# Moving the transposes of k, q and y from TensorE to VectorE seven units earlier (y: six), in an mLSTM cell with a multiplicative FFN

One core of a Trainium2 chip. The metric is the device time of one execution in microseconds (us), the median of several; lower is better.

## The reference

An mLSTM cell (4 batches, 8 heads, 768 positions, head size 40) feeds a feed-forward block without a nonlinearity but with a product of two projections. The cell's data are float32. The weights of the block come as 64-bit floats; the kernel reads them as pairs of 32-bit words and computes in float32.

```python
for t in range(S):                                    # the cell, per batch and head
    m_new  = max(f_gate[t] + m, i_gate[t])
    f_stab = exp(f_gate[t] + m - m_new);  i_stab = exp(i_gate[t] - m_new);  m = m_new
    C = f_stab * C + i_stab * outer(v[t], k[t])       # 40 x 40 state
    n = f_stab * n + i_stab * k[t]
    y[t] = sigmoid(o_gate[t]) * (C @ q[t]) / max(abs(n @ q[t]), 1)

x = y as (B*S, H*D) = (3072, 320)
out = (((x @ w1) * (x @ w2)) @ w3) @ w_out            # 320 -> 1024 -> 1024 -> 320
```

## The kernel before

The sequence is cut into 24 units of 128 rows of one batch. The cell is computed by blocks: for every unit TensorE forms scores from k and q, products with v, and state updates. Because w3 and w_out have nothing between them, the kernel first multiplies them (`wp`: one 128 x 320 block per step from turned words of w3), and uses `w3o = w3 @ w_out` for all rows.

k, q and y of every unit are turned (transposed) ahead of TensorE's products with them, and the kernel has two ways of doing it. In the first, TensorE transposes through PSUM (`pt` for k and q, 1.02 us for eight, `px` for y, 0.33 us for three, in step 13) and ScalarE copies the result out (0.59, 0.59 and 0.50 us). In the second, VectorE turns them (1.09 us for k and for q, 0.57 for y); for that k and q are loaded a second time as rows in a special layout, and y makes a trip through DRAM. `N_DVE` and `NY` say from which unit on the second way is used.

The weights come in pieces of words. For each piece ScalarE scales the upper words, and VectorE makes float32 numbers of it in four instructions (a conversion); a piece of w3 is turned by a fifth.

```python
N_DVE = 17                                   # k, q: VectorE from unit 17 on
NY = 15                                      # y: VectorE from unit 15 on
# one home for the rows, in the memory of the gates:
turned_in = [gates[:, i * TB:(i + 1) * TB] for i in range(2)]

def turn(n):                                 # cut
    if n >= N_DVE:
        for src, dst, name in zip(turned_in, (kT_t, qT_t), ("kT", "qT")):
            dst[n] = sb.tile([128, NP, P], FP, name=name, tag=name)
            nc.vector.transpose(out=..., in_=...)
        return
    ...                                      # TensorE: 8 transposes, 2 copies by ScalarE

def convert():                               # one piece of words on VectorE (cut)
    if not scaled:
        scale_next()                         # ScalarE: scaling of the raw words, "raw<-raw"
    dst, raw, ko, half = scaled.pop(0)
    ...
    w3 = wst.tile([128, CW], FP, name="w3", tag="w3")
    to_f32(w3, raw)                          # 4 instructions: ex, ma, ma, w
    ...
    nc.vector.transpose(out=w3T_t[ko]..., in_=w3...)
```

The main loop; a pass of it is a step. The order of statements is the order of the program text. The build then decides in which order each engine's instructions are queued, within what the data demands; `tc.issue_after(x)` is an edge that forbids it to queue an instruction ahead of x on the same engine. VectorE works its queue off in order, as the 4.36 us below show, in which it stands with ready work further back in its queue.

```python
for s in range(len(n_up)):                   # cut
    load_u(s + 3); load(s + 2); load_o(s + 2)
    ...
    if 0 < s < N_DVE: turn(s)                # TensorE's way
    if NY <= s - 2 < NU: send(s - 2)         # y out to DRAM
    if N_DVE <= s + 1 < NU: load_turned(s + 1)   # rows of k and q, 8 transfers
    if NY <= s - 2 < NU: get_back(s - 2)     # y back in turned layout
    ...
    open_ups = [up(*x) for x in now]         # the projections pa, pb
    gated = quarter_work(s, rest)            # rest(): end of pa, pb and VectorE's product ab;
                                             # then the cell, h, den, y on VectorE
    with tc.issue_after(gated.ins):
        if NY <= s - 2 < NU: x_turn(s - 2)   # VectorE turns y
        if N_DVE <= s + 1 < NU: turn(s + 1)  # VectorE turns k and q
    ...
    for _ in range(n_cvt[s]): convert()      # 2 pieces in each of steps 9 to 15, then none
    while todo and fetched < converted + (2 if s < 2 else 3):
        fetch(*todo.pop(0))                  # words of weights, from DRAM
```

## Time and profile before

| | before |
|---|---|
| median time of the first three executions | 474.29 us (473.12 to 476.47) |
| span of the profiled run | 474.2 us |
| TensorE busy | 450.0 us, 95% of the span |
| VectorE busy | 241.0 us, 51% |
| start of wp's first product in step 10 and in step 17 | 120.20 and 237.69 us |

The lines that say most (chain, steps, groups) stand in the prediction. Two more lines of the page will be wanted, TensorE's busy time and the granted clock in tenths of full speed over 40 slices of the span:

```profile
PE 450.0 (95%) x5375; PEld 362.3 (76%) x5375; DVE 241.0 (51%) x501; ACT 142.4 (30%) x390; POOL 84.2 (18%) x156
...
PEclk9995999999999999999999999999999999999999
```

The change acts in the steps 10 to 17, and the **wp interval**, from the start of wp in step 10 to its start in step 17, holds what it does there, 237.69 - 120.20 = 117.49 us.

### The profile page before, as it was taken

How to read it: one execution, taken by the hardware profiler on the slowest of the kernel's cores; microseconds unless marked ns; L12 is line 12 of the kernel's file. 1: busy time of each engine (PE TensorE's matmuls, PEld its weight loads, DVE VectorE, ACT ScalarE, POOL GpSimd, SP SyncE). 2: the span in 40 equal slices, each digit the busy share in tenths (PEclk: the TensorE clock that was granted, in tenths of full speed). 3: DMA queues.
4: the chain of work that ended last, by engine and by line, in shares of the span. 5: the costliest groups of instructions: out<-in, count | busy, mean ns of one | idle time of the engine just before them, and what ended most of it. 6: DMA issues, size and time to landing. Idle time of an engine off the chain costs nothing.

```text
span 474.2 us, 12856 instructions
## 1 busy us (share of the span) xinstructions
PE 450.0 (95%) x5375; PEld 362.3 (76%) x5375; DVE 241.0 (51%) x501; ACT 142.4 (30%) x390; POOL 84.2 (18%) x156
## 2 busy tenths in 40 slices
PE   2867999899999999999999999999999999999997
PEld 2766878788878888788878787787877778768864
DVE  6676698988865766785351523515236043111110
ACT  3643545544243263344331212211101111011111
POOL 5341333521220222213220211100000000000000
PEclk9995999999999999999999999999999999999999
DMA  7999978599987756432452546354240220200001
GB/s 174 181 166 173 214 138 157 118 201 194 185 165 111 167 104 149 85 65 55 82 121 61 122 105 136 58 127 88 61 116 11 53 43 20 62 14 15 1 15 41
DMA packets 135770, 49.28 MB, mean 104 GB/s; under 512 B 116320, under 2 KB 126752, under 8 KB 135712
## 3 DMA queue, kind: packets, MB, share of 16 engines
q1 hardware_dynamic: 132112, 44.42, 47.8%
q10 hardware_dynamic: 3600, 4.03, 2.5%
q8 instruction: 42, 0.69, 0.6%
q14 instruction: 16, 0.13, 0.1%
HBM read 42.63 MB, written 5.80 MB: 102 GB/s over the span
## 4 chain that ended last, share of the span: by engine, by line
PE 82%; DVE 7%; issue 7%; POOL 2%; ACT 1%; DMA 0%; SPq 0%; DVEq 0%; POOLq 0%
PE pa L90 23%; PE po L90 22%; PE pb L90 16%; PE cell L90 9%; PE wp L90 7%; PE pt L93 2%; DVE h L371 1%; PE ub L90 1%; ACT pw L277 1%; PE px L93 1%; DVE o_in L381 1%; POOL state L306 1%; DVE y L383 1%; DVE h L367 1%; DVE den L378 1%
## 5 line engine op out<-in xcount | busy, mean ns | idle before, releaser
L567 DVE TENSOR_TENSOR ab<-pb,a_sb 128x512 f32<-128x512 f32 x48 | 33.1, 691 | 159.8 <-ACT a_sb L566 159.6
L90 PE MATMUL po<-w3o,ab 128*128 128x320 f32 x384 | 106.2, 435 | 0.0
L90 PEld LDWEIGHTS po<-w3o,ab 128*128 128x128 f32 x384 | 72.1, 190 | 30.1 <-issue 0.4
L90 PE MATMUL pa<-xT,w 128*128 128x256 f32 x384 | 91.1, 380 | 0.6 <-ACT xT L421 0.6
L90 PE MATMUL pb<-xT,w 128*128 128x256 f32 x384 | 90.8, 379 | 0.0
L90 PEld LDWEIGHTS pa<-xT,w 128*128 128x128 f32 x384 | 72.3, 190 | 13.3 <-ACT xT L421 1.0
L90 PEld LDWEIGHTS pb<-xT,w 128*128 128x128 f32 x384 | 72.9, 190 | 10.2 <-ACT kT L296 0.3
L566 ACT ACTIVATE a_sb<-pa 128x512 f32<-128x512 f32 x48 | 28.6, 595 | 149.4 <-PE pb L90 149.4
L90 PE MATMUL pa<-xT,wr 64*64 64x256 f32 x384 | 47.0, 383 | 0.0
L90 PE MATMUL pb<-xT,wr 64*64 64x256 f32 x384 | 47.0, 383 | 0.0
L277 ACT ACTIVATE pw<-pw,aT 128x64 f32<-128x64 f32 x160 | 40.8, 338 | 18.1 <-DMA pw<-U_d 18.1
L279 POOL TENSOR_SCALAR_AFFINE_SELECT pw<-pw 64x512 f32<-64x512 f32 x48 | 35.8, 745 | 52.5 <-ACT pw L277 51.0
L306 POOL TENSOR_TENSOR state<-state,decay 128x164 f32<-128x164 f32 x40 | 19.5, 491 | 139.7 <-issue 53.6
L90 PEld LDWEIGHTS pa<-xT,wr 64*64 64x64 f32 x384 | 25.8, 132 | 16.8 <-issue 7.8
L90 PE MATMUL wp<-wo,w3T 128*128 128x320 f32 x128 | 35.8, 432 | 0.0
L574 ACT COPY o_sb<-po 128x320 f32<-128x320 f32 x24 | 10.2, 423 | 76.6 <-PE po L90 76.4
L90 PEld LDWEIGHTS cell<-vbuf,pw 64*64 64x64 f32 x768 | 27.7, 142 | 6.2 <-issue 2.0
L90 PEld LDWEIGHTS wp<-wo,w3T 128*128 128x128 f32 x128 | 23.7, 190 | 8.9
L90 PE MATMUL cell<-vbuf,pw 64*64 64x41 f32 x768 | 27.6, 232 | 2.4 <-issue 1.4
L347 DVE TENSOR_TENSOR pw<-cell,pw 128x512 f32<-128x512 f32 x24 | 16.5, 686 | 21.7 <-PE cell L90 21.7
L90 PEld LDWEIGHTS pb<-xT,wr 64*64 64x64 f32 x384 | 25.8, 132 | 0.0
L371 DVE TENSOR_TENSOR h<-cell,h 64x328 f32<-64x328 f32 x48 | 23.8, 497 | 1.1
(88 smaller groups left out, 463.4 us busy)
## 6 DMA issues: line engine op xcount, KB each, us to landing
raw<-in_moe_w_dram SPq DMA_DIRECT2D x64, 128.0 KB, 3.2
pw<-U_d SPq DMA_DIRECT2D x40, 128.0 KB, 4.1
kbuf<-in_k_dram SPq DMA_DIRECT2D x24, 160.0 KB, 4.6
vbuf<-in_v_dram SPq DMA_DIRECT2D x24, 160.0 KB, 5.0
o_in<-in_o_gate_dram SPq DMA_DIRECT2D x24, 160.0 KB, 3.7
out_dram<-o_sb ACTq DMA_DIRECT2D x24, 160.0 KB, 2.0
raw<-in_moe_w_dram SPq DMA_DIRECT2D x7, 512.0 KB, 6.0
qbuf<-in_q_dram SPq DMA_DIRECT2D x17, 160.0 KB, 5.0
```

The source lines that it names most:

```text
L90: in_order(nc.tensor.matmul(out, lhsT=lhsT, rhs=rhs, start=start, stop=stop))
L93: in_order(nc.tensor.transpose(out, in_, ident[0:n, 0:n]))
L277: nc.scalar.activation(out=pw[:, h, :], in_=src[:, h, :], func=AF.Exp, bias=aT[:, c, b * H + h:b * H + h + 1])
L279: nc.gpsimd.affine_select(out=pw[r], in_=pw[r], compare_op=OP.is_ge, fill=0.0, base=0, pattern=[[0, H], [1, L]], channel_multiplier=-1)
L306: nc.gpsimd.tensor_tensor(out=new, in0=old, op=OP.mult, in1=decay[:, b * NP:(b + 1) * NP, 2 * c + x:2 * c + x + 1] .to_broadcast([P, NP, D1]))
L347: first_read = nc.vector.tensor_tensor(out=pv, in0=ss, in1=pv, op=OP.mult)
L367: nc.vector.tensor_tensor(out=h.rearrange("p (n two) d -> p two n d", two=2), in0=pi, in1=gT[:, c, hs].rearrange("p (n two) -> p two n", t ...
L371: nc.vector.tensor_tensor(out=h[r], in0=ph[x], in1=h[r], op=OP.add)
L378: nc.vector.tensor_scalar(out=den, in0=den, scalar1=1.0, scalar2=2.0, op0=OP.max, op1=OP.mult)
L566: nc.scalar.mul(out=a_sb, in_=pa, mul=UP ** -2)
L567: nc.vector.tensor_tensor(out=ab_t[gr][j][:, fs[0]:fs[-1] + 1, t0:t0 + a_sb.shape[-1]], in0=pb, in1=a_sb, op=OP.mult)
L574: nc.scalar.copy(out=o_sb, in_=po)
```

## The change

VectorE has time free (51% busy) while TensorE is full (95%), so the transposes of seven more units of k and q (10 to 16) and six more of y (9 to 14) go to VectorE. Three things come along so that the transfers should not stand in the way: the rows alternate between two homes (the gates' memory, and the q buffers, which stand idle by then), y is sent at the end of SyncE's step, and words are fetched two pieces ahead from step 9 on, and no longer three.

```diff
-    N_DVE = 17
-    qbuf = [const.tile([P, H, DP], FP, name=f"qbuf{i}") for i in range(NBQ)]
+    N_DVE = 10
+    q_all = const.tile([P, NBQ * H * DP], FP, name="q_all")
+    qbuf = [q_all[:, i * H * DP:(i + 1) * H * DP].rearrange("p (h d) -> p h d", d=DP) for i in range(NBQ)]
...
-    NY = 15
+    NY = 9
...
-        for dst, src in zip(turned_in, (k, q)):                  # in load_turned; turn() likewise
+        for dst, src in zip(turned_in[n % 2], (k, q)):
...
-    turned_in = [gates[:, i * TB:(i + 1) * TB] for i in range(2)]
+    turned_in = [[mem[:, i * TB:(i + 1) * TB] for i in range(2)] for mem in (gates, q_all)]
...
     for s in range(len(n_up)):
+        if N_DVE <= s + 1 < NU:
+            load_turned(s + 1)
         if B <= s + 3 < NU:
             load_u(s + 3)
...
-        if NY <= s - 2 < NU:
-            send(s - 2)
-        elif 0 <= s - 2 < NY:
+        if 0 <= s - 2 < NY:
             twice(s - 2)
-        if N_DVE <= s + 1 < NU:
-            load_turned(s + 1)
...
-        while todo and fetched < converted + (2 if s < 2 else 3):
+        while todo and fetched < converted + (3 if 2 <= s < 9 else 2):
             fetch(*todo.pop(0))
             fetched += 1
+        if NY <= s - 1 < NU:
+            send(s - 1)
```

More of the change, by code (lines that the diff above doesn't have):

```diff
@@ L285, in turn @@
         if n >= N_DVE:
-            for src, dst, name in zip(turned_in, (kT_t, qT_t), ("kT", "qT")):
+            for src, dst, name in zip(turned_in[n % 2], (kT_t, qT_t), ("kT", "qT")):
                 dst[n] = sb.tile([128, NP, P], FP, name=name, tag=name)
```

## The prediction

> **What bounds the kernel now.** I call one pass of the main loop a step; unit n (128 rows of one batch) passes through the cell's score part in step n and its output part in step n+1. I read the page first, then the chain in order of time, then the busy times by step, then the groups and the waits of SyncE's queue. On the page:
>
> ```profile
> PE 82%; DVE 7%; issue 7%; POOL 2%; ACT 1%; DMA 0%; SPq 0%; DVEq 0%; POOLq 0%
> PE   2867999899999999999999999999999999999997
> ...
> DVE  6676698988865766785351523515236043111110
> ```
>
> The first line is the chain that ended last; the two others are busy tenths in slices of 11.9 us. From the eighth slice on (about 94 us) TensorE is full. Before that the chain runs over VectorE, but none of that work belongs to a unit that the change touches. The chain in order of time shows what a full step is made of. First step 13, then step 19:
>
> ```profile
> 170.29 1.02 PE pt L93 x8
> 171.31 0.33 PE px L93 x3
> 171.64 4.31 PE wp L90 x16
> ...
> 184.74 2.32 PE cell L90 x123
> 187.06 1.02 PE pt L93 x8
> ```
> ```profile
> 281.81 8.81 PE po L90 x32
> ...
> 299.41 2.32 PE cell L90 x123
> 301.73 8.81 PE po L90 x32
> ```
>
> Columns: start, length, what. Step 13 lasts 187.06 - 170.29 = 16.77 us, step 19 lasts 301.73 - 281.81 = 19.92. Step 19 has VectorE turn k, q and y already; if I exchange its 8.81 of po for the 4.31 of wp, 15.42 is left, and 16.77 - 15.42 = 1.35 = 1.02 (eight transposes of k and q) + 0.33 (three of y). So a TensorE step closes up without loss where the transposes are taken out, and 1.35 us is their whole price per step. One step has more:
>
> ```profile
> 135.78 0.48 PE pt L93 x3
> 136.26 0.76 issue
> 137.01 0.75 PE pt L93 x5
> ```
>
> Step 11 loses 17.73 - 16.77 = 0.96 us among its transposes.
>
> Busy time by step (TensorE, weight loads, VectorE, ScalarE, GpSimd, then clock, DMA share and GB/s), steps 9 to 16:
>
> ```profile
> 106.55:119.01 12.46, 12.46 (x204) 10.77 (x205) 11.08 (x24) 5.92 (x16) 2.10 (x4) 1.00 0.99 194
> 119.01:135.78 16.77, 16.77 (x221) 13.81 (x221) 12.25 (x26) 5.91 (x15) 2.73 (x6) 1.00 0.98 175
> 135.78:153.51 17.73, 16.98 (x221) 13.79 (x221) 11.54 (x24) 6.75 (x20) 3.91 (x6) 1.00 0.72 138
> 153.51:170.29 16.78, 16.78 (x221) 13.82 (x221) 11.77 (x25) 6.95 (x20) 3.25 (x7) 1.00 0.55 121
> 170.29:187.06 16.77, 16.77 (x220) 13.81 (x221) 11.88 (x25) 6.57 (x18) 4.78 (x9) 1.00 0.71 149
> 187.06:203.83 16.77, 16.77 (x220) 13.81 (x221) 11.40 (x23) 6.39 (x17) 5.03 (x8) 1.00 0.44 89
> 203.83:220.60 16.77, 16.77 (x220) 13.81 (x221) 11.13 (x23) 7.07 (x18) 3.67 (x6) 1.00 0.25 47
> 220.60:237.37 16.77, 16.77 (x220) 13.81 (x221) 8.65 (x18) 7.71 (x24) 5.47 (x9) 1.00 0.49 95
> ```
>
> TensorE has no hole but the one in step 11; VectorE has 4 to 5 us free per step; the DMA engines are full in steps 9 and 10 and have room later.
>
> [...] each TensorE turn is followed by a ScalarE copy out of PSUM (0.59 us for k, 0.59 for q), and on VectorE's way k and q come in rows loaded twice for the second block, and y goes through DRAM. [...] So SyncE[...] stands where y's way back waits for y's way out, and where a transfer waits for a buffer; in the old kernel its o_gate load stands up to 5.1 us for y in the later steps. [...] this trace has no repeated hole on TensorE.
>
> **The change, part by part.**
>
> ```profile
> L288 DVE STREAM_TRANSPOSE qT<-gates 128x512 f32<-128x512 f32 x7 | 7.6, 1090 | 0.0
> L288 DVE STREAM_TRANSPOSE kT<-gates 128x512 f32<-128x512 f32 x7 | 7.6, 1089 | 0.0
> ...
> L407 DVE STREAM_TRANSPOSE xT<-yb 128x384 f32<-128x384 f32 x9 | 5.1, 572 | 6.3 <-DMA yb<-y_d 6.3
> ```
>
> 1. k and q of units 10 to 16 leave TensorE: 7 steps (10 to 16) of 1.02 = 7.14 us, all on the path.
> 2. y of units 9 to 14 leaves TensorE: in steps 12 to 16 5 x 0.33, and 0.48 in step 17 (from the chain) = 2.13 us.
> 3. The 0.96 us hole of step 11 stands between instructions that are gone. I count half of it as gain, 0.5, since whatever delayed that instruction may delay the next.
> 4. VectorE gets 2 x 1.09 = 2.18 us in each of steps 10 to 16 and 0.57 in steps 12 to 17 (work queued at the end of a step runs in TensorE's next one). Against the shorter steps (15.75 us for steps 10 and 11, 15.42 after) this makes 12.25 + 2.18 = 14.43 (92%), 13.72 (87%), 11.77 + 2.75 = 14.52 (94%), 14.63 (95%), 14.15 (92%), 13.88 (90%), 11.40 (74%). It fits, but with 0.8 to 1.3 us to spare, of which the wait for GpSimd's state product (0.6 to 1.5 us per step) takes nearly all.
> 5. How late may VectorE be? After the change a step takes five banks (wp, pa, pb, pa, pb) of four. The product ab, ready to run about 2.3 us before the step's end, frees the bank that the first pa of the next step takes, after 4.31 us of wp: VectorE has some 6.6 us of room. Before, the q turn took that bank about 2.8 us after the product could start. So taking the turns out also loosens the bank that VectorE frees. The cell's accumulator is wanted again some 13 us after it is full, and the turned k and q some 15 us after the step's beginning; VectorE should have them by about 8.
> 6. SyncE gets 8 loads of turned rows (1.84 us per four in the trace), 4 sends (1.26 + 1.17) and 4 fetches back (1.85), and loses one q load. With u, k, v and o_gate (2.4) and two pieces of words (8 x 0.42) this is 3.68 + 2.43 + 1.85 + 2.4 + 3.4 = 13.8 us of 15.42 in steps 12 to 16. The two homes make the loads independent of the turn just before. With words only two pieces ahead, the word buffer that is refilled was emptied a step earlier; with three, SyncE stood for VectorE (8 waits, 17.2 us in steps 8 to 17), and the send behind it would have stood too. So I expect these two parts to keep SyncE out of the path, with no gain of their own.
> 7. DMA: 1024 packets of 640 B take the place of 1024 of 160 B for q (k and q together); y adds some 2000 short ones. Steps 12 to 16 have the room (0.25 to 0.71 busy). In the full steps 9 and 10 one piece of words fewer is fetched.
> 8. ScalarE loses about 1.7 us per step and GpSimd 0.34, both off the path.
>
> Sum: 7.14 + 2.13 + 0.5 = 9.8 us off; I put 0.4 us back for a few short stands of TensorE behind a VectorE that is over 90% busy: 474.29 - 9.8 + 0.4 = **464.9 us**.
>
> **Rivals.** (a) VectorE becomes the bound in steps 10 to 15. For it: 94 to 95% busy plus the GpSimd wait leaves nothing over, and step 9 was already 11.08 of 12.46. If each of six steps ran 0.7 us over, the room of 6.6 us would absorb most of it; if the words' conversions come late enough to hold wp, 3 to 5 us come back: 468 to 470. Against: the load falls from step 14 on, and wp uses a piece one step after it is turned. (b) SyncE or the loads become late: 13.8 us of 15.42[...] with a send that waits for y. VectorE would then stand for the turned rows and TensorE for VectorE. This would show as waits on the loads of the rows and make 468 or more. Against: the old kernel's later steps do the same without words and no turn of k or q waits at all (0.0 above), and rows are needed about 7 us after they would land by the sum of part 6. (c) Full gain: the hole goes, nothing stands, 474.29 - 7.14 - 2.13 - 0.96 = 464.1. (d) The turns were hidden and nothing is gained: the comparison of steps 13 and 19 speaks against it.
>
> **Range and chances.** Case (c), or close to it, sets the low end; run noise is about 0.3% (473.12 to 476.47 before), so 463.2. A partial (a) or (b) of 3 us sets the high end, 468.0. The limit of 2% is 474.29 x 0.98 = 464.8, right at the estimate: 45% faster, 54% same, 1% slower.
>
> **What would show each step right or wrong.** Right: a chain in which steps 12 to 15 are 15.4 us apart with no transposes of k, q or y, 10 units of TensorE turns left and 9 of y; 14 VectorE turns each of k and q at 1.09 us and 15 of y at 0.57; VectorE over 90% busy in steps 10 to 14 while TensorE stays at 100%; nobody waiting for the turned rows. Wrong: TensorE waiting for ab, a copy of pa or the turned k and q (rival a); VectorE waiting for the rows in either home or for y's way back (rival b); a new hole of about 1 us near step 11, which would say that the old one was not of the transposes; or a front part (up to 106 us) that moved, which I take to be unchanged.

## The result

The changed kernel is slower: **515.64 us** (514.94 to 516.05) against 475.38 us (473.12 to 477.48, four executions) for the kernel before, ratio 1.085 [1.079, 1.090]. Results are correct. Ratios here and below are the mean time of one kernel's fast runs over that of the other's fast runs of the same rounds, so they are not quite the ratio of the medians quoted.

Where the time went, by the wp interval: it is 275.52 - 120.95 = 154.57 us and was 117.49, so 37.1 of the 39.5 us by which the span grew (513.7 against 474.2) lie in the steps 10 to 17. The front part starts step 10's wp 0.75 us later, and 1.7 us come after. First the page of the changed kernel (chain, busy times, TensorE's tenths, its clock, and the group that waits most):

```profile
PE 455.7 (89%) x5301; PEld 363.8 (71%) x5301; DVE 261.0 (51%) x521; ACT 132.4 (26%) x370; POOL 81.1 (16%) x150
...
PE   3858999899599695949586999999999999999997
...
PEclk9975999899989987979797999999999999999999
...
PE 73%; DVE 8%; issue 6%; SPq 4%; DMA 3%; POOL 2%; ACT 2%; DVEq 0%; ACTq 0%; POOLq 0%
...
L90 PE MATMUL cell<-qT,kT 40*64 40x64 f32 x768 | 22.0, 258 | 36.5 <-DVE qT L289 33.3
...
L90 PE MATMUL wp<-wo,w3T 128*128 128x320 f32 x128 | 45.5, 519 | 0.0
```

From slice 11 to slice 22 six digits of TensorE fall to 4 to 6. The score products `cell<-qT,kT` stood idle for 36.5 us, 33.3 of them released by VectorE's turn of q. Second, the clock row now has gaps in these slices or the next ones: over the wp interval the granted clock is 0.89, and it was 1.00. And one product of wp takes 519 ns on average (432 before). TensorE executes 74 instructions fewer than before and is busy 5.7 us longer: 450.0 before, 455.7 now. So the loss has two parts, **waits for the turned q** and **a TensorE that runs slower afterwards**.

Third, the turn itself. TensorE and VectorE in step 12 of the changed kernel (start, length, what; in brackets idle time before it and what ended it):

```profile
174.38 0.67 PE L90 MATMUL cell<-vw,kbuf 64*64 64x41 f32 x30
179.47 1.00 PE L90 MATMUL cell<-qT,kT 40*64 40x64 f32 x32 [4.43 <-DVE qT L289]
180.40 5.89 PE L90 MATMUL wp<-wo,w3T 128*128 128x320 f32 x16
```
```profile
165.18 0.49 DVE L384 TENSOR_TENSOR y<-h,o_in 128x320 f32<-128x320 f32 x1
165.59 0.42 DVE L187 TENSOR_SCALAR ex<-raw 128x512 uint32<-128x512 uint32 x1
...
173.03 0.69 DVE L568 TENSOR_TENSOR ab<-pb,a_sb 128x512 f32<-128x512 f32 x1 [4.36 <-ACT a_sb L567]
...
175.16 0.68 DVE L568 TENSOR_TENSOR ab<-pb,a_sb 128x512 f32<-128x512 f32 x1
...
176.84 0.71 DVE L239 STREAM_TRANSPOSE w3T<-w 128x512 f32<-128x512 f32 x1
177.48 1.04 DVE L289 STREAM_TRANSPOSE kT<-gates 128x512 f32<-128x512 f32 x1
178.36 1.05 DVE L289 STREAM_TRANSPOSE qT<-gates 128x512 f32<-128x512 f32 x1
```

VectorE finishes y at 165.7 us. It could turn k and q there and then, and the rows are in their home: the issues of q's rows are these.

```profile
152.03 1.85 SPq L135 DMA_DIRECT2D gates<-in_q_dram  x4
```

That is 25 us ahead of the turn, such a load lands 2.4 us after its issue (median), and no turn of k or q in the changed kernel has idle time in front of it. (The chain above also names SyncE, 4%, and DMA, 3%. But in the wp interval VectorE stood 33.4 us in front of ab for a_sb, 8.9 us in front of conversions for ScalarE's scaling, and for no rows.) But the turns come last, at 177.48: after the first conversion, after 4.36 us in which VectorE *stands idle*, after the next step's two products ab and the second conversion. In the kernel before, the place was another (step 19):

```profile
286.37 0.49 DVE L383 TENSOR_TENSOR y<-h,o_in 128x320 f32<-128x320 f32 x1
...
287.28 1.07 DVE L288 STREAM_TRANSPOSE kT<-gates 128x512 f32<-128x512 f32 x1
...
299.23 0.69 DVE L567 TENSOR_TENSOR ab<-pb,a_sb 128x512 f32<-128x512 f32 x1 [9.95 <-ACT a_sb L566]
```

There the turns follow y at once. The difference is in the queue, not in the time at which anything is ready: VectorE stood idle for 4.36 us in front of ab, with the turns and their rows ready behind it. This is VectorE's queue as the builds contain it (steps 9 to 16), one row per step, from the score product of the unit to that of the next (P score product, s state, h and y outputs, the dots the denominators, c and w begin and end of a conversion with its dots between, A product ab of the next step, K, Q, X the turns of k, q and y):

```
         before                         changed                        changed, order fixed (e5, below)
step  9  Psshhh....yc...wc...wAAc...w   Psshhh....cy...wc...wAAc...wKQ Psshhh....yKQc...wc...wAA
step 10  Psshhh....yc...wAc..A.w        Psshhh....yc...wKAQA           Psshhh....yKQc...wc...wAA
step 11  Psshhh....yc...wc.A..Aw        Psshhh....yc...wAc..A.wKQ      Psshhh....yKQc...wc...wAA
step 12  Psshhh....yc...wc...wAA        Psshhh....yXc...wAAc...wKQ     PsshXhh....yKQc...wc...wAA
step 13  Psshhh....cy...wc...wAA        Psshhh....yXc.A..Awc...wKQ     PsshXhh....yKQc...wc...wAA
step 14  Psshhhc.......wyc...wAA        Psshhh....yXc...wAAc...wKQ     PsshXhh....yKQc...wc...wAA
step 15  Pscsh.hh....w..yAA             Psshhh....yXc.A..Awc...wKQ     PsshXhh....yKQc...wc...wAA
step 16  Psshhh....yKQAA                Psshhh....yXKQAAX              PsshXhh....yKQXAA
```

In the kernel before, no turn of k and q ever shared a step with a conversion: the conversions end with step 15, and the first turn is in step 16. In the changed kernel they share seven steps, and in six of them the build put K and Q behind everything. The exception, the row of step 10 (`KAQA`), is the one without a wait: step 11, whose unit it turns, takes 16.7 us (wp at 143.13, then at 159.84), and step 12 after it, with the turns last, takes 20.6 (wp at 180.40).

### The profile page after: what moved, and what is told of

Its sections match the earlier page's. It is cut to its first block, busy times and chain, and to the rows that moved or that the text cites. A ratio compares the mean times of both kernels' runs of the same rounds, so it can differ in the third digit from the quotient of the medians.

```text
span 513.7 us, 12839 instructions
## 1 busy us (share of the span) xinstructions
PE 455.7 (89%) x5301; PEld 363.8 (71%) x5301; DVE 261.0 (51%) x521; ACT 132.4 (26%) x370; POOL 81.1 (16%) x150
## 4 chain that ended last, share of the span: by engine, by line
PE 73%; DVE 8%; issue 6%; SPq 4%; DMA 3%; POOL 2%; ACT 2%; DVEq 0%; ACTq 0%; POOLq 0%
PE pa L90 22%; PE po L90 21%; PE pb L90 15%; PE cell L90 7%; PE wp L90 7%; SPq L171 2%; PE pt L93 1%; ACT pw L278 1%; DMA raw<-in_moe_w_dram 1%; DVE kT L289 1%; DVE h L372 1%; PE ub L90 1%; SPq L135 1%; DVE qT L289 1%; POOL pw L280 1%
## 5 line engine op out<-in xcount | busy, mean ns | idle before, releaser
L90 PEld LDWEIGHTS pa<-xT,w 128*128 128x128 f32 x384 | 73.0, 192 | 13.4 <-ACT xT L422 1.0
L90 PEld LDWEIGHTS pb<-xT,w 128*128 128x128 f32 x384 | 73.0, 190 | 10.1 <-ACT kT L297 0.3
L90 PE MATMUL cell<-qT,kT 40*64 40x64 f32 x768 | 22.0, 258 | 36.5 <-DVE qT L289 33.3
L90 PE MATMUL wp<-wo,w3T 128*128 128x320 f32 x128 | 45.5, 519 | 0.0
L90 PEld LDWEIGHTS cell<-qT,kT 40*64 40x64 f32 x768 | 18.3, 164 | 37.5 <-DVE qT L289 34.0
L90 PEld LDWEIGHTS wp<-wo,w3T 128*128 128x128 f32 x128 | 29.3, 235 | 13.2 <-issue 6.1
L280 POOL TENSOR_SCALAR_AFFINE_SELECT pw<-pw 64x512 f32<-64x512 f32 x48 | 33.7, 703 | 20.5 <-ACT pw L278 14.9
```

Source lines behind the costliest of these rows:

```text
L90: in_order(nc.tensor.matmul(out, lhsT=lhsT, rhs=rhs, start=start, stop=stop))
L280: nc.gpsimd.affine_select(out=pw[r], in_=pw[r], compare_op=OP.is_ge, fill=0.0, base=0, pattern=[[0, H], [1, L]], channel_multiplier=-1)
```

## The experiments

Each is a build of its own, correct unless the text says otherwise. (Of the kernel before, two executions in the rounds of e1 to e4 and three in those of e17 and e18 were slow and are left out.) For each the ratio to the kernel before of the same rounds, with its 95% interval, and the wp interval (117.49 before, 154.57 changed).

### 1. Undo one part, or do one part alone

**e3_kq_alone**: the kernel before with the part of k and q alone. **e4_y_alone**: with the part of y alone.

```diff
# e3_kq_alone, against before        # e4_y_alone, against before
+    N_DVE = 10                      +    NY = 9
+    two homes, rows loaded first    +    y sent at the end of the step
```

> Only the k and q part of the change (VectorE turns from the 11th unit on, two homes, rows asked for first in the step); y from the 16th unit on as before, y sent as before, words three pieces ahead as before. VectorE's queue as built has the turn behind both products and a conversion again. Theory A: TensorE's wait for the turned q is nearly as large as in the changed kernel (25-40 us) and the time is 500-515 us. If instead y's way through SyncE is what costs: about 466-470 us.

> Only the y part: y from the 10th unit on through VectorE, sent at the end of SyncE's step; k and q turned on TensorE up to unit 16 and words three ahead as before. Theory A: no harm, the 2.1 us of TensorE's y transposes come off at most: 472-476 us. If y's way is the cause of the loss: above 490 us, with TensorE or VectorE waiting for y's way back.

Measured: e3 512.35 us, 1.084 [1.078, 1.091], wp interval 154.34. e4 484.55 us, 1.023 [1.019, 1.027], interval 121.91. The part of k and q has the whole loss by itself, with the same wait ("PE cell" for "DVE qT", 27.4 us in 6 waits). The part of y costs on its own as well. TensorE's first pa of a step waited twice for y's turn of an earlier unit. VectorE's queue had it behind h, den and y of the step's own unit, the second time with a conversion spread among them; from TensorE's timeline of e4:

```profile
215.18 2.02 PE L90 MATMUL pa<-xT,w 128*128 128x256 f32 x8 [3.01 <-DVE xT L407]
```

### 2. Does the place alone cost time? The kernel before with late turns

**e2_late_turn** adds no work to the kernel before: it only puts the turns of units 17 to 23 behind the second ab of the step that uses them (two homes, so that the rows are not overwritten).

```diff
-            if N_DVE <= s + 1 < NU:
-                turn(s + 1)
...
             for x in open_ups:
-                up_rest(*x)
+                ab = up_rest(*x)
+            if N_DVE <= s < NU:
+                with tc.issue_after(ab.ins):
+                    turn(s)
```

> The kernel BEFORE, with its turns of k and q of units 17 to 23 moved behind the second product ab of the step that uses them (two homes for the rows, so that the later turn does not read overwritten rows). No work is added; VectorE is only about 40% busy there. Theory A: TensorE waits for the turned q in each of these 7 steps; the second ab ends 0.6 us before TensorE reaches the score products and the turns take 2 us, so about 1.5-2.5 us a step, perhaps more if the clock falls: 486-495 us against 475. Theories B and C (late rows, or too much work): no such wait, within 1% of before.

Measured: 496.79 us, 1.048 [1.041, 1.055]; span 495.1, 20.9 us more than before; the wp interval, which lies ahead of the moved turns, is unchanged (117.43). So a late place costs time with no work added. TensorE waited 7 times, 10.5 us in all. The other half is slower running: TensorE is busy 461.0 us with the same 5375 instructions as before, 11.0 us more. One of the steps, in TensorE's timeline of e2:

```profile
286.70 0.69 PE L90 MATMUL cell<-qT,kT 40*64 40x64 f32 x32 [1.51 <-DVE qT L289]
287.32 10.57 PE L90 MATMUL po<-w3o,ab 128*128 128x320 f32 x32
```

After the wait of 1.5 us the 32 products of po take 10.50 us by the chain. They took 8.81 before. That happened after 5 of the 7 waits, and the granted clock over these products is 0.84; after the other two po took 8.81, at a clock of 1.00.

### 3. Take the turns forward: only the turns

**e1_turn_first** is the changed kernel with one edge more: whatever VectorE is given after the turns stays behind them.

```diff
+    first = ExitStack()
     for s in range(len(n_up)):
...
+            first.close()
             if N_DVE <= s + 1 < NU:
-                turn(s + 1)
+                ins = turn(s + 1)
+                first.enter_context(tc.issue_after(ins.ins))
```

> The changed kernel with one edit: everything that VectorE gets after the turn of k and q in program order (conversions of words, the products ab of the next step) is queued behind that turn. Nothing else differs in the program. Theory A (place in VectorE's queue: the rows had landed some 20 us before they were turned, the turn stood behind both products ab and a conversion): TensorE's waits for the turned q (33.3 us in six steps in the changed kernel) fall under 5 us, the wp products that follow fall back from 5.5-6.4 us to about 4.3 us, and the time falls from 515.6 to 463-469 us. Theory B (SyncE is late with the rows): VectorE now waits for the rows at the turn, several us a step, TensorE still waits for the turned q, time above 490 us. Theory C (VectorE simply has too much work): TensorE waits for other VectorE results (ab, state) instead, time 475-500 us.

Measured: **528.26 us**, 1.116 [1.111, 1.120], interval 166.06. This expectation failed, and usefully. The waits for q are gone, but the build now put the first piece's conversion behind and between the next step's work (`P.swcs.h.h.hwX....yKQcA.A.` in the letters of above): VectorE does one instruction of it after the turns, stands idle for ab (5.83 us in step 12's turn), and then spreads the rest into the following step. TensorE's wp stands for the words instead:

```profile
PE wp L90 <- DVE w3T L239: 36.9, 5, 7.6
```

(us in all, times, longest). It is the same fault with another victim: not enough of the order was fixed.

### 4. Fix the whole order

**e5_order_fixed** is the changed kernel with e1's edge and a second one behind each conversion, so that VectorE's queue is turns, both conversions, both ab, as in the third column above. No work, buffer or transfer differs from the changed kernel.

```diff
             ins = convert()
             converted += 1
+            if s >= N_DVE - 1:
+                first.enter_context(tc.issue_after(ins.ins))
```

> The changed kernel with VectorE's queue put, by order edges alone, into the order that the prediction assumed: after y the turns of k and q, then both conversions of words, then both products ab. (The first such run fixed only the turns; the build then put the rest of the first conversion behind both products, and TensorE waited 7 us a step for the w3 block.) Theory A (order in VectorE's queue is the whole loss): TensorE's waits for the turned q and for the w3 block both go below 1 us a step, clock back to 0.98 or above, 463-468 us. Theory C (VectorE has too much work, whatever the order): TensorE waits for the products ab or their banks or the cell's results in steps 10 to 15, 470-490 us. Theory B (SyncE/words late): VectorE's idle times name the words, the rows or y's way back, and 475-500 us.

**e5_kq_only** is the same for the part of k and q alone (`NY = 15`, y sent as before, words three ahead). **e5_words3** is e5_order_fixed with words three ahead.

> As the run before it but only the k and q part (y as in the kernel before: from the 16th unit on, sent as before; words three ahead). Theory A: 465-469 us (7.1 us of turns and perhaps the 0.96 us hole of step 11 off). If it is better than the run with y, then y's way costs more than its 2.1 us; if the run with y is better, y pays.

> As the first of these three, but words three pieces ahead at every step, as in the kernel before. If the words two pieces ahead are what keeps SyncE out of the way (as the prediction held), this run is slower by several us, with SyncE standing for VectorE's conversions; if two pieces make the conversions wait for their words, this run is faster. Else within 0.5% of the first.

Measured:

| | median, us | ratio | wp interval |
|---|---|---|---|
| e5_order_fixed | 473.83 | 0.993 [0.990, 0.996] | 115.58 |
| e5_kq_only | 469.05 | 0.982 [0.978, 0.986] | 111.28 |
| e5_words3 | 474.87 | 0.995 [0.990, 1.000] | 115.02 |

The order alone takes back 41.6 us of the changed kernel's span (513.7 to 472.1): TensorE's busy time falls from 455.7 to 442.0 with the same 5301 instructions (13.7 us of slower running), the rest of its span from 58.0 to 30.1 (27.9 us of waits). From the page of e5_order_fixed:

```profile
PE 442.0 (94%) x5301; PEld 354.1 (75%) x5301; DVE 256.4 (54%) x521; ACT 132.4 (28%) x370; POOL 82.0 (17%) x150
...
PEclk9995799999999999999999999999999999999999
```

Nearly all of it lies in the wp interval: 27.4 us of waits and 11.6 of slower running, and the granted clock there is 1.00 again. This settles the main cause. It also clears rows, SyncE and the amount of VectorE's work of the 40 us, since e5 has all of them unchanged. The time itself missed what was expected of it (463 to 468 us), for a reason that follows below.

e5_kq_only shows what the transposes of k and q were worth. All of its steps 10 to 16 last 15.90 us, step 11 too, and TensorE has no hole in them. The step was 16.77 long; so 0.87 us come out seven times (six in the wp interval, and once just ahead of it for unit 10), and the 0.96 us hole of step 11 is gone: 7.05, against 474.2 - 467.2 = 7.0 by the spans. The price of eight transposes is thus 0.87 and not 1.02: with them gone, y's three cost 0.48 each step where they had cost 0.33.

e5_words3 is not apart from e5_order_fixed: with this order alone, two pieces of words ahead show no gain over three.

In the whole change a loss remains: from step 13 on the steps of e5_order_fixed are 17.14 us long, though the sum said 15.42. Two views, the waits and ScalarE's timeline:

```profile
DVE ex L187 <- ACT raw L176: 10.1, 4, 2.7
...
PE wp L90 <- DVE w3T L238: 5.9, 4, 1.5
```
```profile
196.68 0.60 ACT L567 ACTIVATE a_sb<-pa 128x512 f32<-128x512 f32 x1 [7.00 <-issue]
197.18 0.66 ACT L176 ACTIVATE raw<-raw 128x512 f32<-128x512 f32 x1
```

VectorE stands 2.4 us for the second piece's scaling on ScalarE, and the scaling sits behind the copy a_sb of the next pa, which is ready only at 196.68. Either that is again an order, now in ScalarE's queue, or the words are late because SyncE issues without a pause in these steps.

### 5. Is SyncE, or are the loads, what is left?

Four kernels relieve SyncE, all on top of e5_order_fixed. **e8_q_rows_by_scalar** and **e9_rows_by_scalar** have ScalarE issue q's rows or all rows, **e11_y_back_by_scalar** y's fetch back. **e12_half_rows** leaves out four of the eight row loads of units 12 to 16; its result is wrong (relative error 0.363).

```diff
-                    nc.sync.dma_start(out=dst[p0:p0 + 32, ...                              # load_turned
+                    (nc.scalar if src is q else nc.sync).dma_start(out=dst[p0:p0 + 32, ... # e8
+                    nc.scalar.dma_start(out=dst[p0:p0 + 32, ...                            # e9
-            nc.sync.dma_start(out=back_t[n][32 * i:32 * (i + 1)]...                        # get_back
+            nc.scalar.dma_start(out=back_t[n][32 * i:32 * (i + 1)]...                      # e11
-                for j in range(2):                                                         # load_turned
+                for j in range(1 if 12 <= n < 17 else 2):                                  # e12
```

> The order-fixed kernel (turns, conversions, products) with the 4 loads of q's rows per unit issued from ScalarE's queue instead of SyncE's; also an order edge that keeps k's turn ahead of q's. In the order-fixed run SyncE issues without a pause, 17.1 us a step, and TensorE's steps are 17.14 us with a 1.5 us wait for the w3 block whose words land late. If SyncE's issuing is what bounds those steps, 4 x 0.45 = 1.8 us less of it makes them 15.4-15.9 us and the time 464-468 us against 474. If VectorE's load (about 15.1 us of work and unavoidable waits a step) bounds them, the time stays within 2 us of 474.

> As the run before it, with all 8 row loads per unit from ScalarE's queue (3.7 us less for SyncE, 3.7 us more on ScalarE, which is some 30% busy). If SyncE bounds: 464-468 us, as good as the run before it or better; one turn of y stands behind the products ab in this build, so one wait of some 2 us of TensorE for xT is possible. If ScalarE[...] suffers (its copies of pa late): TensorE waits for a_sb, above 468.

> As the order-fixed run, with the 4 fetches back of y per unit issued from ScalarE's queue (1.85 us less for SyncE, and its wait for y's turn moves to ScalarE). If SyncE bounds: 464-468 us. If ScalarE stands for y's turn and so delays its copies: 468-480 us.

> WRONG RESULT ON PURPOSE: the order-fixed kernel (473.8 us) without the second-block loads of the rows of k and q for units 12 to 16 (the turns then read old rows there). VectorE does exactly the same work in the same order; SyncE issues 4 loads fewer per step (1.8 us) and 512 packets of 640 B fewer move. If SyncE and the transfers (17.1 us of issuing a step without a pause) bound steps 12 to 16 of the order-fixed kernel: TensorE's 1.5 us waits for the w3 block go, steps 15.4-15.9 us, 465-469 us. If VectorE's amount of work bounds them: no change, 472-475 us.

| | median, us | ratio | wp interval |
|---|---|---|---|
| e8_q_rows_by_scalar | 481.54 | 1.012 [1.006, 1.018] | 122.65 |
| e9_rows_by_scalar | 486.99 | 1.024 [1.018, 1.030] | 126.81 |
| e11_y_back_by_scalar | 479.27 | 1.008 [1.001, 1.016] | 119.26 |
| e12_half_rows | 472.74 | 0.992 [0.988, 0.995] | 115.58 |

Moving the issues made it worse in all three. In e8, SyncE needs up to 7.21 us, waits included, for the four fetches of y that took 2.07 to 2.30 in e5_order_fixed (the view of waits names the loads of q's rows for 16.9 us of its standing there), and rows came later (VectorE's turn of k waited up to 4.0 us for them). So SyncE's fetches grew by up to 4.9 us in e8, while it was spared the issues of q's rows (1.85 us); which queue stood for which was not followed up. These three builds also have an edge that keeps k's turn ahead of q's, and y's turn has another place in them (in e9 once behind both ab, where TensorE waited 2.1 us for it), so not all of their loss need come from the issues. e12 is the clean test. SyncE pauses there, with fewer loads, and the wp interval is 115.58 us, to the hundredth that of e5_order_fixed, with the same 5.9 us in 4 waits for w3T. So SyncE was not the bound of e5_order_fixed.

### 6. The order in ScalarE's queue

**e14_scalar_order_too** adds an edge on ScalarE: the scaling of both pieces ahead of the next step's copies of pa. **e15_both_words3** is the same with words three ahead.

```diff
-        nc.scalar.activation(out=hi, in_=hi, func=AF.Prelu, ...)         # scale()
+        return nc.scalar.activation(out=hi, in_=hi, func=AF.Prelu, ...)
...
-        scale(scaled[-1][1])
+        scales.append(scale(scaled[-1][1]))
...
                 first.enter_context(tc.issue_after(ins.ins))
+                first.enter_context(tc.issue_after(scales[-1].ins))
```

> The order-fixed kernel (473.8 us, ratio 0.993) with one more kind of order edge: on ScalarE the scaling of both pieces of words goes ahead of the next step's copies of pa. In the order-fixed run, steps 13 to 16 are 17.14 us; the words of a step's second conversion were asked for a whole step earlier, but their scaling stands behind the first copy of pa in ScalarE's queue, so VectorE stands 2.4 us, the conversion and the products end late and TensorE waits 1.5 us for the w3 block. If that place in the queue is what is left of the loss: no such wait, steps of 15.4-15.6 us, time 464-467 us, ratio 0.975-0.980, which was the prediction's estimate. If VectorE's amount of work (about 15.1 us a step with its waits) or SyncE (17.1 us of issuing a step) is the bound after all: steps stay at 16-17 us, 469-473 us.

> The same with words three pieces ahead at every step, as in the kernel before. If two pieces ahead are needed for SyncE (prediction, part 6): slower than the run before it by over 1%. If not: within 0.5% of it.

Measured: e14 469.80 us, 0.985 [0.982, 0.988], interval 111.11. e15 473.56 us, 0.994 [0.990, 0.998], interval 113.93. The wait of VectorE for the scaling is gone, and the steps 12 to 15 are 15.62 us long. By the trace the place in the queue was thus the cause up to step 15; by the time e14 falls into the range expected for the other case (469 to 473), because of step 16. The chain of e14:

```profile
149.58 4.50 PE wp L90 x16
165.20 4.50 PE wp L90 x16
...
196.43 4.50 PE wp L90 x16
229.21 6.23 PE wp L90 x16
```

One hole is left, 1.55 us before the wp at 229.21, followed by a slow wp (6.23). Here VectorE's turn of k waited 2.12 us for its rows, and the chain leads back over them to SyncE. SyncE's cycle in e14 is 18.2 and then 18.0 us (its fetches of y start at 168.77, 186.96 and 204.96), so it falls behind TensorE by some 2.5 us per step until it is late at step 16. Words two ahead are worth 2.8 us of the wp interval once both orders are fixed (the ratios are 0.9% apart, but the profiled run of e15 had also started step 10 by 3.6 us later): with three, TensorE stood twice for w3T in e15 (2.6 us), and the last three intervals between wps are 16.7 to 17.3 us.

### 7. Which part of the change is worth keeping?

**e13_y_from_14th**: k and q as in e5_order_fixed, y from unit 13 on only, words three ahead, e5's order. **e17_y_from_12**: e14 with y from unit 12 on. **e18_kq_both_orders**: e14 with y as in the kernel before.

```diff
-    NY = 9
+    NY = 13    # e13
+    NY = 12    # e17
+    NY = 15    # e18, and send(s - 2) at its old place
```

> The best version tried: k and q on VectorE from the 11th unit with the fixed order, and y on VectorE only from the 14th unit, whose sends fall into steps in which SyncE has few or no words left to fetch. The k-and-q-only version with fixed order had a ratio of 0.982. y's transposes cost 0.48 us a step on TensorE when they stand alone, so two fewer are worth 1.0 us at most: ratio 0.979-0.984. If y's way costs SyncE even there, 0.984-0.990.

> The changed kernel with both orders fixed, but y turned by VectorE only from unit 12 on instead of 9. SyncE has no sends before unit 12, so it should not be late at step 16 to the same degree. If SyncE's backlog builds up over the steps with sends (18.2 us per step against 15.6), the hole of 1.55 us before wp at step 16 becomes smaller than 1 us or goes, while steps 12 to 14 get 0.48 us back for y's transposes: 0.982 to 0.986. If the lateness is set by each step alone, the hole stays and the time is 0.986 to 0.989.

> The part of k and q alone, with y as in the old kernel, words two pieces ahead, and the order fixed on VectorE (turns, then both conversions, then both products ab) and on ScalarE (both scalings ahead of the next step's copies of pa). What it tells apart: whether, once the order on both engines is fixed, y's part is worth anything. If TensorE sets the pace, steps 12 to 16 have y's transposes back (0.48 us each) and this lies near e5_kq_only (0.982) and e14 (0.985): steps of 15.9 us, no hole at step 16, since SyncE is free of sends: 0.980 to 0.984, 465 to 468 us. If y's part is a gain that SyncE's lateness at step 16 of e14 hid, it is slower than e14: 0.987 to 0.99.

| | median, us | ratio | wp interval |
|---|---|---|---|
| e13_y_from_14th | 469.46 | 0.985 [0.981, 0.989] | 110.62 |
| e17_y_from_12 | 469.88 | 0.988 [0.982, 0.993] | 110.33 |
| e18_kq_both_orders | 470.12 | 0.988 [0.983, 0.994] | 111.28 |

e17 has no hole at step 16 and the shortest interval, 0.95 us shorter than that of e18 with no y in it. Its steps are 15.90 us long with y's transposes and 15.62 without, so y is worth 0.28 us per step. SyncE's lateness is one that builds up: with the sends and fetches of three units fewer before it, it does not show. (By its ratio, 0.988, e17 falls into the range expected for the other case, 0.986 to 0.989; it is the trace that decides here.) In the whole times these three, e14 and e5_kq_only are not apart. Their gain of 1.2 to 1.8% over the kernel before is shown in every one of them, though by the limit of 2% four of them count as the same, and e5_kq_only, whose interval reaches over 2%, as unclear.

The spans gain less than the intervals: e17 wins 117.49 - 110.33 = 7.2 us there and 0.87 before it (unit 10), together 8.0, but its span is only 6.3 shorter. The difference lies ahead of the interval: e17 starts step 10's wp at 121.03 us, 0.83 later than the kernel before and not 0.87 earlier; from step 17 on the two take equally long (236.5 us). In general the start of wp in step 10 moved between 118.10 us (e14) and 121.70 (e15) over the variants with the order fixed, whose front parts do the same work. The granted clock ahead of that wp was 0.94 and 0.89 in these two runs, so TensorE's clock in the front part differs; whether that is the whole of it was not tested.

## Why the prediction was wrong

- **The step that failed** is in part 5: "VectorE should have them by about 8". It asked whether VectorE has enough *time* for the turns, and never where in its *queue* they would stand. The turns of units 12 and 13 began 17.6 and 20.0 us after the step's wp (177.48 - 159.84 and 200.35 - 180.40), although VectorE stood idle for over 4 us of that. What stood behind the sentence was the kernel before, in whose later steps the turns follow y directly; but those are the steps without conversions. The evidence did not cover the new case, and rival (b) drew its comfort ("the old kernel's later steps do the same without words and no turn of k or q waits at all") from the same steps. Shown by e5_order_fixed: order alone, 41.6 us.
- **A second term is missing from the sum**: what a wait costs on TensorE after it has ended. In the changed kernel wp after a wait of 4.43 us takes 5.82 us and not 4.31 (granted clock 0.77 over it), and in e2 po takes 1.69 us longer after 5 of 7 waits of 1.5 us (granted clock 0.84). How the cost depends on the length of a wait was not shown. This term is 13.7 us between the changed kernel and e5_order_fixed. The prediction's rival (a) let "3 to 5 us come back" in all and put nothing on top.
- **The prices of part 1 and 2** were somewhat too high: k and q are worth 0.87 per step (e5_kq_only) and y 0.28 (e17), in place of 1.02 and 0.33, together 1.15 and not 1.35. The kernel before has the first in its own chain: the step without k and q but with y (221.79 to 237.69) is 15.90 long. The second was hidden by the exchange of po for wp: the 4.31 us are those of a wp that follows y's transposes, and without them, straight after the cell, it takes 4.50 (e14). The step is then 15.62 and not 15.42.
- **Part 3**, the hole of step 11: taken as half a gain. It goes completely with the transposes in every variant with the order fixed (15.90 us in e5_kq_only).
- **Part 4**, VectorE very busy and still in time: right, though it was 13.0 to 13.4 us busy in steps 12 to 15 of e14 (83 to 86%), where the sum had 13.9 to 14.6 (90 to 95%). (The "4 to 5 us free per step" before were read loosely too: the lines shown give 4.5 to 8.1 in steps 10 to 16 and 1.4 in step 9.) In e14 it has 0.46 and 1.26 us idle in a step of 15.62 (before the score product and for GpSimd's state), and TensorE does not wait in steps 12 to 15. Rival (a), VectorE as the bound, named waits that came; but their cause was order and not load.
- **Part 6**, SyncE: 13.8 us was too low. (In the kernel before, SyncE stood 4.2 us, in 5 waits, with y's way back for y's way out.) The cycle is 18.0 to 18.2 us in e14, with its waits. In the one that starts at 186.96, k's four row loads took 3.20 us (I had 1.84), u, k, v and o_gate together 3.7 (2.4), the eight transfers of words 3.66 (3.4), and some 1 us lay between the issues. It stopped no turn in the changed kernel, where steps were longer; it is the next bound once the order is fixed. That words two ahead help shows once both orders are fixed (e14 against e15), and not before (e5_words3).
- **Rows and transfers**: right as far as asked. No turn of k or q waited for its rows in the changed kernel (0.0 us of idle time in front of the four groups of turns).

Left open: by which rule the build placed the turns behind the conversions and ab; the runs show the queues, not the reasons. Also why the front parts, up to step 10, differ by up to 3.6 us.

## What to carry to other kernels

Before moving work to an engine that "has time", ask where in that engine's queue it will stand, and whether the steps you take as evidence have the same neighbours as the steps you change; here VectorE stood idle for 4.36 us in front of the next step's ab with the ready turns behind it, and the order alone was worth 41.6 us. When the build chooses the order, fix it whole: an edge on one instruction pushed the fault on to the next (e1: 36.9 us of waits for w3T), and the same fault then sat in another engine's queue (10.1 us of VectorE's waits for the scaling in e5_order_fixed, gone in e14). Count a TensorE wait as possibly more than its length (here 13.7 us of slower running on top of 27.9 us of waits), and cut the steps at a product that all variants have (here wp), which tells apart variants that whole times do not.

## Short waits, and issues from two engines

- Waits of 1.5 us were followed by slow products, 10.50 us of po where 8.81 is usual, after 5 of 7 waits in e2, and by a wp of 6.23 us after one of 1.55 us in e14; while four waits of 1.44 to 1.49 us in e5_order_fixed were followed by a wp of 4.54 us each, at a granted clock of 1.00. So a short wait can cost about 1.7 us more, and not every one does.
- e8, e9 and e11 were 1.5 to 3.1% slower than e5_order_fixed by the ratios, with issues moved to ScalarE (and y's turn in another place). In e8 SyncE's four fetches of y took up to 7.21 us while ScalarE issued the rows of q, in place of 2.07 to 2.30.
